# The first block's queries in two halves by heads, one load of a round's last keys with a filled upper half, and a new early order

## The chip, the cores and the metric

The kernel runs on one core of one Trainium2 chip. The metric is the device time of one execution in microseconds (us). Three executions of the kernel before took 822.5, 821.15 and 820.46 us; the median is 821.15. TensorE (PE, with its weight loads as PEld), VectorE (DVE), ScalarE (ACT) and GpSimd (POOL) each run their own queue of instructions in order; SyncE (SP) issues most of the loads and all stores. A change of less than 0.3% (2.5 us) can't be told from none here.

## The reference

Three layers follow each other: linear attention, a gated convolution, and a channel mix with a squared ReLU. Batch 8, 576 positions, 8 heads of 64, so a model width of 512; the hidden width is 1024.

```python
q_s = softmax(q, axis=-1)                  # over the 64 values of a head
k_s = softmax(k, axis=2)                   # over the 576 positions
kv  = einsum('bhsd,bhse->bhde', k_s, v)    # 64x64 for each head
x   = einsum('bhsd,bhde->bhse', q_s, kv)   # then (batch, 576, 512)
gate = sigmoid(sum_k conv_w[k] * x shifted by 4 - k)     # 5 taps, causal
y    = (gate * (x @ w_val)) @ w_out
xk, xr = mixes of y and y shifted by one, with mu_k and mu_r
out  = sigmoid(xr @ w_r) * (relu(xk @ w_k)**2 @ w_v)
```

The weights come as 64-bit numbers; the kernel loads them as pairs of 32-bit words and puts a 32-bit number together from each.

## The kernel before

**Blocks.** The 8 x 576 positions are cut into 12 blocks of T = 384. Each block goes through `V` (times w_val, 4 steps), `Y` (w_out), `R` (w_r), `H` (w_k, 8 steps) and `A` (w_v, 8 steps). Block 0 multiplies plain 32-bit numbers (`whole` weights). From block 1 on each operand is split into a high and a low part and three products are summed.

**Rounds.** The keys and values of four heads of one batch element are a round; there are 16. A round loads its keys (`k_load`: 512 positions as 128 x 4, then the last 64) and values (`v_load`), takes the maximum over positions on DVE (`kv_max`, tile `pm`, its last step over the last 64 positions), turns it with PE (`pmT`, reduced to `m`), spreads it over partitions with PE (`mx`), subtracts it on DVE and takes the exponential on ACT (`kv_exp`), and multiplies keys by values on PE (`kv_mm`, tile `kvacc`). A ones column in the values gives the sums (`den`), and DVE writes the 64x64 matrices (`kvf`). The last 64 positions fill half of the 128 partitions; the other half is loaded with the same keys a second time and its values are zeros. So round 0 gives heads 0 to 3 of the first batch element and round 1 heads 4 to 7.

**Queries.** `load_q` loads a block's queries, for block 0 into `came` (768 KB, in one load). `q_exp` and `q_norm` make the softmax of all 8 heads at once: a maximum (`qm`), a subtraction, an exponential on ACT, a sum (`qs`), a reciprocal and a product. `x_turn` turns two heads (`pq` on PE, `q` by ACT), `x_chunk` multiplies them by `kvf` (`px`, then `xf` by ACT), and `x_gate` makes the gate (one step on ACT, four on DVE, a tanh on ACT). There are four chunks, 0 to 3: chunks 0 and 1 need round 0 alone, chunks 2 and 3 need round 1.

**Weights.** 28 chunks of 512 KB come through seven buffers `raw`: six for most, and one for those in `LEFT_WEIGHTS`. A chunk is put together (`decode`) by one instruction on ACT and two on DVE (`raw<-raw`, then `whole<-raw`), and only then is its buffer free for the next load. In blocks 0 and 1 the weights are also split into high and low parts, once.

**Order.** All is written out in the order of the table `FRONT`, up to block 2's queries: `lwout0` loads chunk 0 of w_out, `wout0` decodes it, `swout0` splits it, `lk0`, `max0`, `turn0` and `mm0` are round 0, `qexp.0` is block 0's `q_exp`, `xturn0.0`, `x0.0` and `gate0.0` its chunk 0, `V0.0` its first step of V (`pv`), `gf0.0` the gate's product with it. A scheduler then places each engine's instructions, so the order on an engine can differ from the table. From block 2 on the table `REST` puts the side work behind the main steps. SP issues loads in its own order too, and at most eight loads are out at a time: each waits for the one eight before it.

Of the kernel before, what the change touches and what calls it, by code (L numbers as in the profile page):

```python
# [8 lines left out]
F32 = mybir.dt.float32  # L9
# [3 lines left out]
ALU = mybir.AluOpType  # L13
AX = mybir.AxisListType
# [3 lines left out]

FRONT = (
# [12 lines left out]
).split()  # L34
REST = {
    0: "max0",
# [19 lines left out]

CONV_ON_TENSOR = ()

LEFT_WEIGHTS = "wval1 wout2 wr2 wr3 wk2 wk7 wv2".split()


@with_exitstack
def tile_linear_attention_gated_conv_channel_mix(
# [15 lines left out]
    nc = tc.nc  # L79
    B, H, S, D = q.shape  # L80
# [4 lines left out]
    P = 128  # L85
    NC = DM // P
    NF = DFF // P
    T = 384
    NT = T // P
    NB = B * S // T  # L90
    NS4 = 4
    KT = NS4 * P
    TAIL = S - KT
    NST = NS4 + 1
    HR = 4
# [5 lines left out]
    odd = ctx.enter_context(tc.tile_pool(name="odd", bufs=1))  # L101
    wts = ctx.enter_context(tc.tile_pool(name="wts", bufs=1))
    kvp = ctx.enter_context(tc.tile_pool(name="kvp", bufs=1))
    work = ctx.enter_context(tc.tile_pool(name="work", bufs=1))
# [11 lines left out]
    first = first_ctx.enter_context(tc.tile_pool(name="first", bufs=1))  # L116
# [6 lines left out]
    def f32(ap):  # L123
        return ap.bitcast(F32)
# [81 lines left out]
    def load_weight(n):  # L206
        w, (kc, c0) = CHUNKS[n]
        here = n in LEFT_WEIGHTS
        raw = raws[n] = (first if here else early).tile([P, WC, 2], U32, tag="raw", bufs=1 if here else 6, name="raw")
# [49 lines left out]

    def frame(vt):
        nc.gpsimd.memset(vt[:, :, 0:NS4, D:VW], 1.0)
        nc.gpsimd.memset(vt[:TAIL, :, NS4, D:VW], 1.0)
        nc.gpsimd.memset(vt[TAIL:P, :, NS4, :], 0.0)
# [3 lines left out]
    vt1 = first.tile([P, HR, NST, VW], F32, name="vt1")  # L269
    frame(vt)  # L270
    frame(vt1)

    def k_load(st):
        b, j = st["at"]
        src = k[b, HR * j:HR * (j + 1)]
        t = st["k"] = kt1 if st is rounds[1] else work.tile([P, HR, NST, D], F32, tag="kt", bufs=1, name="kt")
        nc.sync.dma_start(
            t[:, :, 0:NS4, :].rearrange("p h s d -> p h (s d)"),
            src[:, 0:KT, :].rearrange("h (p s) d -> p h (s d)", s=NS4),
        )  # L280
        for p in (0, TAIL):
            nc.sync.dma_start(t[p:p + TAIL, :, NS4, :], src[:, KT:S, :].rearrange("h p d -> p h d"))

    def v_load(st):
        b, j = st["at"]
# [86 lines left out]
    def segments(i):  # L372

        t, o, segs = i * T, 0, []
        while o < T:
            b, s = divmod(t + o, S)
            n = min(T - o, S - s)
            segs.append((o, n, b, s))
            o += n
        return segs  # L380


    def load_q(i):
        qt = work.tile([P, NT, H, D], F32, tag="qt", bufs=1, name="qt")
        if i == 0:
            came = first.tile([P, H, NT, D], F32, name="came")
            nc.sync.dma_start(
                came.rearrange("p h t d -> p h (t d)"), q[0, :, 0:T, :].rearrange("h (p t) d -> p h (t d)", t=NT)
            )
            return qt, came  # L390
        for t in range(NT):
            for o, n, b, s in segments(i):
                lo_, hi_ = max(o, t * P), min(o + n, (t + 1) * P)
                if lo_ < hi_:
                    nc.sync.dma_start(
                        qt[lo_ - t * P:hi_ - t * P, t, :, :],
                        q[b, :, s + lo_ - o:s + hi_ - o, :].rearrange("h p d -> p h d"),
                    )
        return qt, None

    def q_exp(qt, came):
        qm = odd.tile([P, NT * H], F32, tag="qm", bufs=1, name="qm").rearrange("p (t h) -> p t h", t=NT)
        src = qt if came is None else came.rearrange("p h t d -> p t h d")
        nc.vector.tensor_reduce(out=qm, in_=src, axis=AX.X, op=ALU.max)
        nc.vector.tensor_sub(qt, src, qm.rearrange("p t (h o) -> p t h o", o=1).to_broadcast([P, NT, H, D]))
        nc.scalar.activation(qt, qt, AF.Exp)

    def q_norm(qt):
        a = qt.rearrange("p t h d -> p (t h) d")
        n = NT * H  # L410
        qs = odd.tile([P, n], F32, tag="qm", bufs=1, name="qs")
        nc.vector.tensor_reduce(out=qs, in_=a, axis=AX.X, op=ALU.add)
        nc.vector.tensor_scalar_add(qs, qs, EPS)
        nc.vector.reciprocal(qs, qs)
        nc.vector.tensor_mul(a, a, qs.rearrange("p (n o) -> p n o", o=1).to_broadcast([P, n, D]))

    def pair_of(tag, bufs, pool=work):
        return lambda name: tuple(pool.tile([P, T], F32R, tag=tag, bufs=bufs, name=name + x) for x in "hl")
# [3 lines left out]
    def one(tag, bufs, name):  # L422
        return (gatep if tag == "g" else work).tile([P, T], F32, tag=tag, bufs=bufs, name=name)
# [32 lines left out]
            nc.gpsimd.tensor_copy(tail, view[:, g - 1, w - tail.shape[1]:w])  # L456

    def x_turn(st, i, c):
        qt = st["qt"][0]
        pq = ps_t.tile([P, 512], F32, tag="t", name="pq")  # L460
        for t in range(NT):
            nc.tensor.transpose(  # L462
                pq[:, t * P:(t + 1) * P], qt[:, t, 2 * c:2 * c + 2, :].rearrange("p h d -> p (h d)"), f32(ident)
            )
        if i < 2:
            qf, = st["q", c] = (one("q", 2, "q"),)
            if i:
                nc.scalar.copy(qf, pq[:, :T])
            else:
                nc.scalar.copy(  # L470
                    qf.rearrange("c (p t) -> c p t", t=NT), pq[:, :T].rearrange("c (t p) -> c p t", t=NT)
                )
            return
        qh, ql = st["q", c] = q_pair("q")
        nc.scalar.copy(qh, pq[:, :T])
        nc.vector.tensor_sub(ql, pq[:, :T], f32(qh))
# [40 lines left out]
    def x_gate(st, i, c):  # L517
        g = len(segments(i))
        L = T // g
        gx = lambda a: a.rearrange("p (g t) -> p g t", g=g)  # L520
        xv = st["xv", c]
        data = xv[:, :, HALO:]
        gate = work.tile([P, T], F32, tag="gate", bufs=4, name="gate")
        st["gate", c] = gate
        if i == 0 and c in CONV_ON_TENSOR:
            nc.scalar.activation(gate, conv_on_tensor(xv, c), AF.Tanh, scale=0.5)
            return
        nc.scalar.activation(gx(gate), data, AF.Copy, scale=tap(c, HALO))
        for sh in range(1, NTAP):
            nc.vector.scalar_tensor_tensor(  # L530
                out=gx(gate), in0=xv[:, :, HALO - sh:HALO - sh + L], scalar=tap(c, HALO - sh),
                in1=gx(gate), op0=ALU.mult, op1=ALU.add,
            )
        nc.scalar.activation(gate, gate, AF.Tanh, scale=0.5)
# [158 lines left out]

    def attention(i, nxt):
        out = {
            "qload": lambda: nxt.update(qt=load_q(i)), "qexp": lambda: q_exp(*nxt["qt"]), "qnorm": lambda: q_norm(nxt["qt"][0]),
        }
        for c in range(NC):
            out[f"xturn{c}"] = lambda c=c: x_turn(nxt, i, c)
            out[f"x{c}"] = lambda c=c: x_chunk(nxt, i, c)  # L700
            out[f"gate{c}"] = lambda c=c: x_gate(nxt, i, c)
        return out
# [23 lines left out]
    with tc.issue_after(cast.ins):  # L726
        for n in FRONT:
            todo_front.pop(n)()
            if n == START:
                break  # L730
    for n in FRONT[FRONT.index(START) + 1:]:
        todo_front.pop(n)()
# [42 lines left out]
```

## Time and profile before

| | us |
|---|---|
| median of three executions | 821.15 |
| the profiled execution, whole | 820.3 |
| its span, first to last instruction | 818.4 |
| PE busy | 794.6 (97%) |
| DVE busy | 562.3 (69%) |
| ACT busy | 481.3 (59%) |
| POOL busy | 48.8 (6%) |

The span is what the profile's rows add up to; 1.9 us of the profiled execution lie around it. Busy times overlap between engines. On one engine the next instruction can start before the last has ended in the records, so the distance from start to start is what an instruction costs its queue. A product of plain 32-bit numbers has two records on PE.

### The profile page before, as it was taken

Reading aid. Unit: us, or ns where it says so; the run is one execution under the profiler, and the core shown is the slowest. Engines: PE = TensorE matmul, PEld = TensorE weight load, DVE = VectorE, ACT = ScalarE, POOL = GpSimd, SP = SyncE. Lnnn points to the kernel's source line nnn. Section 1 sums busy time; section 2 is a strip of 40 time slices with the busy share of each in tenths; the row PEclk is TensorE's granted clock in tenths of the full one; section 3 lists DMA queues with packets and bytes.
Section 4 is the critical chain, followed back from the end, with each engine's and each line's share of the span. In section 5 each row is a group of like instructions: output and inputs, shape, how many; then the busy total and the mean of one; then the engine's idle time right before and its main releaser. Section 6 shows DMA issues by size and latency. Waiting matters only on the chain.

```text
span 818.4 us, 12130 instructions
## 1 busy us (share of the span) xinstructions
PE 794.6 (97%) x4530; PEld 696.3 (85%) x4530; DVE 562.3 (69%) x1010; ACT 481.3 (59%) x947; POOL 48.8 (6%) x208
## 2 busy tenths in 40 slices
PE   2999999999999999999999999999999999999997
PEld 1545577999989999999999999999999998998996
DVE  6987689997658667577658578568675857653611
ACT  4566579646754755754753763773673674564542
POOL 1110011000000001100000100100000100100000
PEclk9999999999999999999999999999999999999999
DMA  9685250322032012111241211211213002000001
GB/s 323 199 270 190 61 140 1 76 64 62 8 93 90 13 38 75 26 40 50 52 100 40 62 40 39 62 39 39 62 47 80 14 1 52 26 0 14 26 1 39
DMA packets 96872, 54.28 MB, mean 66 GB/s; under 512 B 78354, under 2 KB 88622, under 8 KB 96814
## 3 DMA queue, kind: packets, MB, share of 16 engines
q1 hardware_dynamic: 96768, 53.49, 22.8%
q8 instruction: 35, 0.57, 0.3%
q14 instruction: 23, 0.19, 0.1%
q10 hardware_dynamic: 46, 0.02, 0.0%
HBM read 44.06 MB, written 9.44 MB: 65 GB/s over the span
## 4 chain that ended last, share of the span: by engine, by line
PE 93%; DVE 3%; DMA 2%; ACT 1%; issue 0%; SPq 0%; DVEq 0%
PE ph L435 25%; PE vacc L435 25%; PE racc L435 12%; PE py L435 11%; PE pv L435 11%; PE px L435 3%; PE kvacc L340 3%; PE pq L462 2%; DMA raw<-in_moe_w_k_dram 1%; DMA came<-in_q_dram 1%; DVE gate L530 1%; DMA raw<-in_moe_w_r_dram 1%; PE mx L326 0%; PE pmT L314 0%; DVE gf L571 0%
## 5 line engine op out<-in xcount | busy, mean ns | idle before, releaser
L435 PE MATMUL ph<-xkh,wk_hi 128*128 128x384 f32 x352 | 120.9, 344 | 0.0
L530 DVE SCALAR_TENSOR_TENSOR gate<-xf,cw,gate 128x384 f32<-128x384 f32 x192 | 117.2, 615 | 3.5 <-issue 0.8
L435 PE MATMUL ph<-xkh,lower 128*128 128x384 f32 x352 | 118.4, 336 | 0.0
L435 PE MATMUL ph<-xkl,wk_hi 128*128 128x384 f32 x352 | 118.4, 336 | 0.0
L428 DVE TENSOR_TENSOR kl<-rf,kh 128x384 fp32r<-128x384 f32 x88 | 48.9, 555 | 87.2 <-ACT kh L427 86.1
L624 ACT ACTIVATE rf<-ph 128x384 f32<-128x384 f32 x96 | 46.9, 490 | 98.6 <-PE ph L435 98.2
L435 PE MATMUL vacc<-wv_hi,kh 128*128 128x512 f32 x264 | 104.2, 395 | 0.0
L435 PE MATMUL vacc<-lower,kh 128*128 128x512 f32 x264 | 103.2, 391 | 0.0
L435 PE MATMUL vacc<-wv_hi,kl 128*128 128x512 f32 x264 | 102.8, 391 | 0.0
L598 DVE SCALAR_TENSOR_TENSOR xm<-yf,mus,xm 128x384 f32<-128x384 f32 x96 | 56.8, 615 | 25.3 <-ACT xm L597 24.8
L435 PEld LDWEIGHTS ph<-xkh,wk_hi 128*128 128x128 f32 x352 | 66.2, 188 | 2.1
L435 PEld LDWEIGHTS ph<-xkh,lower 128*128 128x128 f32 x352 | 66.2, 188 | 1.8
L435 PEld LDWEIGHTS ph<-xkl,wk_hi 128*128 128x128 f32 x352 | 66.1, 188 | 0.0
L435 PE MATMUL py<-gh,wout_hi 128*128 128x384 f32 x176 | 59.9, 347 | 1.8 <-DVE gf L571 1.8
L435 PE MATMUL pv<-xh,wval_hi 128*128 128x384 f32 x176 | 59.4, 338 | 0.0
L435 PE MATMUL pv<-xh,lower 128*128 128x384 f32 x176 | 59.3, 337 | 0.0
L435 PE MATMUL pv<-xl,wval_hi 128*128 128x384 f32 x176 | 59.0, 337 | 0.0
L435 PEld LDWEIGHTS vacc<-wv_hi,kl 128*128 128x128 f32 x264 | 49.5, 188 | 11.0 <-DVE kl L428 0.3
L435 PE MATMUL py<-gh,lower 128*128 128x384 f32 x176 | 58.0, 336 | 0.0
L435 PE MATMUL py<-gl,wout_hi 128*128 128x384 f32 x176 | 57.6, 337 | 0.0
L597 ACT ACTIVATE xm<-yf,mus 128x384 f32<-128x384 f32 x96 | 55.8, 613 | 2.3 <-DVE xrl L428 0.9
L435 PEld LDWEIGHTS vacc<-wv_hi,kh 128*128 128x128 f32 x264 | 49.6, 188 | 8.1 <-ACT kh L427 0.3
(129 smaller groups left out, 1644.8 us busy)
## 6 DMA issues: line engine op xcount, KB each, us to landing
out_dram<-rs SPq DMA_DIRECT2D x36, 256.0 KB, 2.0
kt<-in_k_dram SPq DMA_DIRECT2D x16, 512.0 KB, 4.5
qt<-in_q_dram SPq DMA_DIRECT2D x29, 256.0 KB, 3.7
vt<-in_v_dram SPq DMA_DIRECT2D x56, 128.0 KB, 3.6
raw<-in_moe_w_k_dram SPq DMA_DIRECT2D x8, 512.0 KB, 7.3
raw<-in_moe_w_v_dram SPq DMA_DIRECT2D x8, 512.0 KB, 4.8
raw<-in_moe_w_out_dram SPq DMA_DIRECT2D x4, 512.0 KB, 3.7
kt<-in_k_dram SPq DMA_DIRECT2D x32, 64.0 KB, 4.0
```

Source lines behind the costliest of these rows:

```text
L340: nc.tensor.matmul(acc[e * D:(e + 1) * D, x * VW:(x + 1) * VW], lhsT=kt[:, 2 * x + e, s, :], rhs=st["v"][:, 2 * x + e, s, :], start=(s == ...
L428: nc.vector.tensor_sub(pair[1], a, f32(pair[0]))
L435: nc.tensor.matmul(po, lhsT=left[a], rhs=right[b], start=start and x == 0, stop=stop and x == len(m) - 1)
L462: nc.tensor.transpose(pq[:, t * P:(t + 1) * P], qt[:, t, 2 * c:2 * c + 2, :].rearrange("p h d -> p (h d)"), f32(ident))
L530: nc.vector.scalar_tensor_tensor(out=gx(gate), in0=xv[:, :, HALO - sh:HALO - sh + L], scalar=tap(c, HALO - sh), in1=gx(gate), op0=ALU.mult ...
L597: nc.scalar.activation(gx(xf), yv[:, :, 0:L], AF.Copy, scale=om[:, c:c + 1])
L598: nc.vector.scalar_tensor_tensor(out=gx(xf), in0=yv[:, :, 1:], scalar=mu[:, c:c + 1], in1=gx(xf), op0=ALU.mult, op1=ALU.add)
L624: nc.scalar.activation(rf, ph[:, :T], AF.Relu)
```

## The change

Block 0's queries are loaded by two loads of four heads each (`qload0.0`, `qload1.0`, 384 KB), and `q_exp` and `q_norm` run once for heads 0 to 3 and once for heads 4 to 7 (`qexp0.0`, `qnorm0.0`, `qexp1.0`, `qnorm1.0`). Later blocks keep all heads at once. The last 64 keys of a round are loaded once, into the lower half; POOL fills the upper half with -3.0e38, whose exponential is zero. `LEFT_WEIGHTS` names other chunks, and `FRONT` is a new table (a part of its first line is shown). Line numbers below are those of each kernel.

```diff
-    "lwout0 lk0 qload.0 lk1 max0 cload lv0 lv1 lwval0 lwval1 lwval2 lwval3 lwout1 lwr0 lwout2 lwout3 qexp.0 turn0 "
+    "qload.0 qload0.0 lk0 cload lwval0 lwval1 lk1 lv0 lv1 lwval2 qload1.0 lwout0 lwout1 lwval3 lwr0 max0 turn0 lwout3 "
...
-LEFT_WEIGHTS = "wval1 wout2 wr2 wr3 wk2 wk7 wv2".split()
+LEFT_WEIGHTS = "wval1 wr0 wk1 wk5 wv2".split()
...
+    LEAST = -3.0e38
...
-        for p in (0, TAIL):
-            nc.sync.dma_start(t[p:p + TAIL, :, NS4, :], src[:, KT:S, :].rearrange("h p d -> p h d"))
+        nc.sync.dma_start(t[:TAIL, :, NS4, :], src[:, KT:S, :].rearrange("h p d -> p h d"))
+        nc.gpsimd.memset(t[TAIL:P, :, NS4, :], LEAST)
...
+    def load_half(st, j):
+        h = slice(j * HR, (j + 1) * HR)
+        nc.sync.dma_start(
+            st["came"][:, h].rearrange("p h t d -> p h (t d)"),
+            q[0, h, 0:T, :].rearrange("h (p t) d -> p h (t d)", t=NT),
+        )
+
+    def q_exp(st, h=slice(0, H)):
+        n = h.stop - h.start
+        qt = st["qt"][:, :, h, :]
+        src = st["came"].rearrange("p h t d -> p t h d")[:, :, h, :] if "came" in st else qt
+        qm = odd.tile([P, NT * n], F32, tag=f"qm{n}", bufs=1, name="qm").rearrange("p (t h) -> p t h", t=NT)
...
+    def q_norm(st, h=slice(0, H)):
...
+        if i == 0:
+            for j in range(2):
+                h = slice(j * HR, (j + 1) * HR)
+                out[f"qload{j}"] = lambda j=j: load_half(nxt, j)
+                out[f"qexp{j}"] = lambda h=h: q_exp(nxt, h)
+                out[f"qnorm{j}"] = lambda h=h: q_norm(nxt, h)
```

On PE, from round 0's product of keys and values (`kvacc<-vt,kt`) to the first products of block 0's V (`pv`), there stood before:

```order
L340 MATMUL kvacc<-vt,kt 64x65 x20
L314 MATMUL pmT<-ident,pm 128x128 x2
L326 MATMUL mx<-ident,m_249 128x128 x2
L462 MATMUL pq<-ident,qt 128x128 x3
L435 MATMUL px<-q,kvf_116 128x384
L340 MATMUL kvacc<-vt_124,kt_123 64x65 x20
L462 MATMUL pq<-ident,qt 128x128 x3
L435 MATMUL pv<-xf,whole 128x384
```

And on the same engine now, a little further on:

```order
L344 MATMUL kvacc<-vt,kt 64x65 x20
L473 MATMUL pq<-ident,qt 128x128 x6
L318 MATMUL pmT<-ident,pm 128x128 x2
L446 MATMUL px<-q,kvf_116 128x384 x2
L330 MATMUL mx<-ident,m_264 128x128 x2
L177 MATMUL pc<-ident,cwt 128x20
L446 MATMUL pv<-xf,whole 128x384
L180 MATMUL pm<-ident,mut 128x8
L446 MATMUL pv<-xf,whole 128x384 x4
L344 MATMUL kvacc<-vt_124,kt_123 64x65 x20
L446 MATMUL pv<-xf,whole 128x384 x3
L473 MATMUL pq<-ident,qt 128x128 x6
```

Chunks 0 and 1 (two `px`) and five products of V moved ahead of round 1's `kvacc<-vt_124,kt_123`; the small transposes of the constants (`pc`, `pm`), which were ahead of round 0, moved behind it.

On ACT, around round 0's exponential (`kt<-kt`) and the copies of the two rounds' values (`vt<-dense`, `vt_124<-dense`), there stood before:

```order
L406 ACTIVATE qt<-qt 128x1536
L176 COPY cw<-pc 128x20
L299 COPY vt<-dense 128x4x4x64
L180 COPY mus<-pm 128x8
L330 ACTIVATE kt<-kt 128x1280
L299 COPY vt_124<-dense 128x4x4x64
L146 ACTIVATE raw<-raw 128x512 x3
```

And now:

```order
L148 ACTIVATE raw<-raw 128x512 x2
L416 ACTIVATE qt<-qt 128x3x256
L303 COPY vt<-dense 128x4x4x64
L303 COPY vt_124<-dense 128x4x4x64
L334 ACTIVATE kt<-kt 128x1280
L148 ACTIVATE raw<-raw 128x512
```

Round 1's copy of values moved ahead of round 0's exponential, and two weight chunks ahead of the queries' exponential, which is for half of the heads.

On DVE, from the sums of round 0 (`den<-kvacc`) to the second round's subtraction (`kt_123<-kt_123,mx`), there stood before:

```order
L347 TENSOR_SCALAR den<-kvacc 128x2
L316 TENSOR_REDUCE m_249<-pmT 128x2
L348 RECIPROCAL den<-den 128x2
L147 TENSOR_SCALAR raw<-raw 128x512
L352 TENSOR_TENSOR kvf_116<-kvacc,den 64x2x64 x2
L327 TENSOR_TENSOR kt_123<-kt_123,mx 128x1280
```

And now:

```order
L351 TENSOR_SCALAR den<-kvacc 128x2
L414 TENSOR_REDUCE qm<-came 128x12
L352 RECIPROCAL den<-den 128x2
L415 TENSOR_TENSOR qt<-came,qm 128x3x256
L356 TENSOR_TENSOR kvf_116<-kvacc,den 64x2x64 x2
L320 TENSOR_REDUCE m_264<-pmT 128x2
L149 TENSOR_SCALAR raw<-raw 128x512
L423 TENSOR_REDUCE qs<-qt 128x12
L149 TENSOR_SCALAR raw<-raw 128x512
L331 TENSOR_TENSOR kt_123<-kt_123,mx 128x1280
```

The second half of the queries now stands between `den` and `kvf`, and behind it; round 1's `m` moved behind `kvf`.

## Rows read from the trace of the kernel before

**Rows 1.** The page: span, and busy time of each engine (share, instructions).

```profile
span 818.4 us, 12130 instructions
PE 794.6 (97%) x4530; PEld 696.3 (85%) x4530; DVE 562.3 (69%) x1010; ACT 481.3 (59%) x947; POOL 48.8 (6%) x208
```

**Rows 2.** Stretches from:to: length; PE, PEld, DVE, ACT, POOL; clock, DMA share, GB/s.

```profile
0.00:27.20 27.20, 11.12 (x98) 7.70 (x99) 18.82 (x37) 12.73 (x19) 4.72 (x28) 1.00 0.86 286
27.20:800.00 772.80, 769.36 (x4368) 676.86 (x4367) 539.72 (x968) 464.49 (x920) 44.06 (x180) 1.00 0.21 59
```

**Rows 3.** A wait of PE in the span: us in total, times, longest.

```profile
PE py L435 <- DVE gf L571: 2.2, 2, 1.8
```

**Rows 4.** PE in order of time: start, us, line, op, tiles, records, idle before.

```profile
16.65 2.44 PE L340 MATMUL kvacc<-vt,kt 128*64 128x65 f32 x40 [2.10 <-issue]
...
22.60 1.65 PE L435 MATMUL px<-q,kvf 128*128 128x384 f32 x2 [0.57 <-ACT q L470]
...
26.54 0.90 PE L462 MATMUL pq<-ident,qt 128*128 128x128 f32 x3
27.24 1.21 PE L435 MATMUL pv<-xf,whole 128*128 128x384 f32 x2
28.28 0.81 PE L435 MATMUL px<-q,kvf 128*128 128x384 f32 x2
...
35.40 5.32 PE L435 MATMUL pv<-xf,whole 128*128 128x384 f32 x16
40.55 5.32 PE L435 MATMUL py<-gf,whole 128*128 128x384 f32 x16
46.26 5.43 PE L435 MATMUL py<-gf,whole 128*128 128x384 f32 x16 [0.38 <-DVE gf L571]
...
52.49 10.57 PE L435 MATMUL racc<-whole,xm 128*128 128x512 f32 x24 [0.59 <-DVE xm L598]
```

**Rows 5.** DVE in order of time, 8 to 53 us.

```profile
8.89 1.75 DVE L404 TENSOR_REDUCE qm<-came 128x24 f32<-128x1536 f32 x1 [1.18 <-DMA came<-in_q_dram]
...
13.76 1.49 DVE L327 TENSOR_TENSOR kt<-kt,mx 128x1280 f32<-128x1280 f32 x1
...
20.49 0.58 DVE L352 TENSOR_TENSOR kvf<-kvacc,den 64x128 f32<-64x128 f32 x2
...
30.61 2.73 DVE L530 SCALAR_TENSOR_TENSOR gate<-xf,cw,gate 128x384 f32<-128x384 f32 x5 [0.24 <-ACT gate L528]
...
35.06 1.29 DVE L148 SCALAR_TENSOR_TENSOR whole<-raw 128x512 uint32<-128x512 uint32 x2
...
45.65 1.02 DVE L571 SCALAR_TENSOR_TENSOR gf<-gate,pv 128x384 f32<-128x384 f32 x2 [1.58 <-ACT gate L534]
46.58 0.69 DVE L148 SCALAR_TENSOR_TENSOR whole<-raw 128x512 uint32<-128x512 uint32 x1
...
51.49 0.43 DVE L147 TENSOR_SCALAR raw<-raw 128x512 uint32<-128x512 uint32 x1 [0.35 <-DMA raw<-in_moe_w_r_dram]
51.83 0.61 DVE L598 SCALAR_TENSOR_TENSOR xm<-yf,mus,xm 128x384 f32<-128x384 f32 x1
```

**Rows 6.** ACT in order of time, 15 to 23 us.

```profile
15.28 1.27 ACT L330 ACTIVATE kt<-kt 128x1280 f32<-128x1280 f32 x1
16.45 1.03 ACT L299 COPY vt<-dense 128x1024 f32<-128x1024 f32 x1
...
22.07 0.48 ACT L470 COPY q<-pq 128x384 f32<-128x384 f32 x1 [2.87 <-PE pq L462]
```

**Rows 7.** SP's issues: round 1's values, and the last chunk of w_r.

```profile
8.88 0.37 SPq L290 DMA_DIRECT2D dense<-in_v_dram  x1
...
47.33 0.33 SPq L210 DMA_DIRECT2D raw<-in_moe_w_r_dram  x1
```

**Rows 8.** From issue to landing: the values, then the page's row on w_k.

```profile
DMA to landing us min/median/max: 5.6/5.6/5.7
...
raw<-in_moe_w_k_dram SPq DMA_DIRECT2D x8, 512.0 KB, 7.3
```

**Rows 9.** POOL in order of time, one fill of the zero half.

```profile
3.83 0.31 POOL L265 MEMSET vt<- 64x260 f32 x1
```

More of the change, by code (lines that the diff above doesn't have):

```diff
@@ L380, in segments, with load_q @@
         return segs
-    def load_q(i):
-        qt = work.tile([P, NT, H, D], F32, tag="qt", bufs=1, name="qt")
+    def load_q(i, st):
+        st["qt"] = work.tile([P, NT, H, D], F32, tag="qt", bufs=1, name="qt")
         if i == 0:
[L386 to L390, printed above, removed]
+            st["came"] = first.tile([P, H, NT, D], F32, name="came")
+            return
         for t in range(NT):
@@ L395, in load_q @@
                     nc.sync.dma_start(
-                        qt[lo_ - t * P:hi_ - t * P, t, :, :],
+                        st["qt"][lo_ - t * P:hi_ - t * P, t, :, :],
                         q[b, :, s + lo_ - o:s + hi_ - o, :].rearrange("h p d -> p h d"),
                     )
[L399 to L403, printed above, removed]
+    def load_half(st, j):
[9 more added lines that the diff above has]
+        qm = odd.tile([P, NT * n], F32, tag=f"qm{n}", bufs=1, name="qm").rearrange("p (t h) -> p t h", t=NT)
         nc.vector.tensor_reduce(out=qm, in_=src, axis=AX.X, op=ALU.max)
-        nc.vector.tensor_sub(qt, src, qm.rearrange("p t (h o) -> p t h o", o=1).to_broadcast([P, NT, H, D]))
+        nc.vector.tensor_sub(qt, src, qm.rearrange("p t (h o) -> p t h o", o=1).to_broadcast([P, NT, n, D]))
         nc.scalar.activation(qt, qt, AF.Exp)
[L408 to L412, printed above, removed]
+    def q_norm(st, h=slice(0, H)):
+        n = h.stop - h.start
+        qt = st["qt"][:, :, h, :]
+        qs = odd.tile([P, NT * n], F32, tag=f"qm{n}", bufs=1, name="qs")
+        q4 = qs.rearrange("p (t h) -> p t h", t=NT)
+        nc.vector.tensor_reduce(out=q4, in_=qt, axis=AX.X, op=ALU.add)
         nc.vector.tensor_scalar_add(qs, qs, EPS)
         nc.vector.reciprocal(qs, qs)
-        nc.vector.tensor_mul(a, a, qs.rearrange("p (n o) -> p n o", o=1).to_broadcast([P, n, D]))
+        nc.vector.tensor_mul(qt, qt, q4.rearrange("p t (h o) -> p t h o", o=1).to_broadcast([P, NT, n, D]))
     def pair_of(tag, bufs, pool=work):
@@ L458, in x_turn @@
     def x_turn(st, i, c):
-        qt = st["qt"][0]
+        qt = st["qt"]
         pq = ps_t.tile([P, 512], F32, tag="t", name="pq")
@@ L695, in attention @@
         out = {
-            "qload": lambda: nxt.update(qt=load_q(i)), "qexp": lambda: q_exp(*nxt["qt"]), "qnorm": lambda: q_norm(nxt["qt"][0]),
+            "qload": lambda: load_q(i, nxt), "qexp": lambda: q_exp(nxt), "qnorm": lambda: q_norm(nxt),
         }
+        if i == 0:
[4 more added lines that the diff above has]
+                out[f"qnorm{j}"] = lambda h=h: q_norm(nxt, h)
         for c in range(NC):
```

23 rows, old and new, of the table FRONT are left out of this document.

## The prediction

> **What bounds the kernel now.** I read the busy row of each engine first: PE is busy for 794.6 of the span's 818.4 us, DVE for 562.3 [rows 1]. Next the stretches, to see where PE's missing time lies: up to 27.2 us PE works for 11.12 us, while from 27.2 to 800 us it works for 769.36 of 772.80 [rows 2]. So the idle time to be won is some 16 us at the front. Of the 3.4 us idle behind 27.2 us, the waits put 2.2 on Y's product waiting for DVE's `gf`, in two places, 1.8 in the longer one (block 1) [rows 3], and 0.59 stands in front of R [rows 4]. Last I read the engines in order of time. PE works on `kvacc` at 16.65, the first `px` at 22.60, the first V product at 27.24, Y at 40.55, R at 52.49 [rows 4]. From there on it is full. The change leaves every matrix product as it was, so its worth is how much earlier or later R starts, if nothing new stands still behind that.
>
> One more thing is to be seen. A `px` of two records took 1.65 us at 22.60 and 0.81 us at 28.28 [rows 4]: half the time, as between TensorE's lower level (1.2 GHz) and its upper (2.4). It rose between those two, after PE had worked without a pause since 22.60. At the upper level eight products go from 35.40 to 40.55, 0.645 us each [rows 4].
>
> **The change part by part.**
>
> *Loads and values.* The first steps of round 0 need its keys, and both kernels must wait for values. The loads issued ahead of round 1's values are, before, 512 + 640 + 768 + 640 + 576 KB; now 384 + 576 + 1024 + 576 + 576 KB; both sums are 3136 KB. Round 1's values were issued at 8.88 [rows 7] and took 5.6 [rows 8], so they landed at 14.5, and I take 14.5 again. What is new is that ACT copies them (1.03 [rows 6]) ahead of round 0's exponential, to 15.5; the exponential takes 1.17 until the next instruction starts [rows 6], so `kvacc` starts at 16.7. It started at 16.65: no gain. Bounds: without the copy in the way, the exponential follows DVE's subtraction, which ended at 15.2 [rows 5]. DVE now handles half of the queries ahead of it but also two steps on a weight chunk; I estimate 14.1 at best, hence `kvacc` from 15.5. If the values land 1 us later, 17.7.
>
> *Queries in halves.* A full `qm` takes 1.75 us for 1536 elements, a subtraction 1.49 for 1280 [rows 5]; by that slope 768 elements take 0.97, by half of 1.75 it is 0.88. Four such DVE steps in two halves each therefore add 0 to 0.8 us, and most of it falls into time in which DVE waits. What counts is where the second half stands: its `qm` and its subtraction now lie between `den` and `kvf`. `kvacc` ends at 16.7 + 2.4 = 19.1; then 0.1 + 0.9 + 0.1 + 0.9 + 0.6 gives `kvf` at 21.7. Before, it ended at 20.49 + 0.58 = 21.1 [rows 5]: 0.6 later.
>
> *Chunks 0 and 1 ahead of round 1's `kvacc`.* Both are turned (`pq` 0.7 us at the lower level [rows 4], the copy 0.48 [rows 6]) while DVE makes `kvf`. PE then has `pmT` (0.7), two `px` at 1.6 each and `mx` (0.7): the first V product starts at 21.7 + 0.7 + 3.2 + 0.7 + 0.1 = 26.4, against 27.24. That is 0.8 earlier, but round 1's `kvacc` (2.4 before) is still to do, and one `px` and one `pq` (0.65 + 0.35 at the upper level) are done already.
>
> *Where it goes.* `kvacc` of round 1 waits for its exponential, which stands on ACT behind the constants' copies, two gate steps and a weight chunk and, on DVE, behind an `mx` that PE reaches only at 25.6. I get the exponential's end at about 30.6. The five products of V ahead of it last from 26.4 to 30.9 if two of them go at the lower level, so PE stands still hardly at all. `kvacc` then ends at 32.2, its three V products at 34.2, `kvf` of round 1 at about 34.1, `pq` and `px` of chunks 2 and 3 with their copies at 36.5, eight products more at 41.7; without the pauses that I see for the copies, 41.1. V ended at 40.55 before. So V is 0.5 to 1.1 us later.
>
> *Y and R.* Y's third row waited until 46.26 for two `gf` [rows 4, 5], 0.56 beyond 40.55 + 5.15. DVE now has put two chunks fewer together by then (a `whole` step is 0.65 [rows 5], so 1.3 us less, and as much more for their first steps); a gate step stays 0.55 [rows 5]. I expect `gf` at 45.0 and Y's third row without a wait, since V ends later by itself. Y ends at 41.1 to 41.7 + 10.3 = 51.4 to 52.0 (before 51.5). R stood behind Y's end by about 0.95, which is the way over ACT and DVE's `xm` at 51.83; I take 0.75, since the step on a w_r chunk that held DVE to 51.83 [rows 5] has moved. R starts at 52.15 to 52.75, and I take 52.3: **0.2 us earlier**.
>
> *Last keys.* Of two loads of 64 KB a round one goes, and a POOL fill of 64 x 256 comes, about 0.31 us by the fill of 64 x 260 [rows 9]; 16 x 0.31 = 5 us on an engine with 48.8 us of work [rows 1]. It waits for the buffer as the load did, and stands ahead of the exponential by whole blocks from round 2 on; in rounds 0 and 1 it runs while the keys are on their way. Price 0; if its cover were gone, 0.31 a round.
>
> *Later blocks.* A few small PE groups stand some products earlier. PE is full there; 0 to 0.3 us either way, taken as 0. Block 1's wait of 1.8 for `gf` stays.
>
> *Sum.* 818.4 - 0.2 = 818.2 in the span, and with the 1.9 around it 820.1. The profiled execution took 820.3, 0.85 under the median, so against the median it is 820.95, say **820.9**.
>
> **The rivals.**
>
> *Faster: an early exponential.* If the values land earlier than at 14.5 because fewer small loads share the queues, `kvacc` starts at 15.5, `kvf` is there at 20.5, PE works without a pause from there, the upper level comes before the second `px` (0.8 saved), and V starts at 24.4. As round 1's exponential moves along, R starts at 50.3 to 49.6: 2.2 to 2.9 less, 818.2 to 818.9. For it: DVE and ACT have less ahead of the exponential. Against it: the same bytes ahead of the values, and a DMA share of 0.86 in this stretch [rows 2].
>
> *Slower: a w_k chunk in R's way.* DVE's first step on wk1 now stands ahead of the first `xm`, and ACT's ahead of the second. Its load goes out when wr0 has been put together, about where that `whole` step was, at 46.6 [rows 5]. The last w_r chunk before was issued at 47.33 [rows 7] and its DVE step waited to 51.49 [rows 5], 4.2; the w_k loads took 7.3 [rows 8]. So it lands at 50.8 or at 53.9. It decides from 51.3 on; at 53.9 the first `xm` comes 2.6 later, R starts at about 55.0, and the time is 823.6. I am nearer to 4.2, because in the new order few loads are out at that time.
>
> *Slower: the level stays low.* What the row shows is that the level rose behind a stretch with `px`, `kvacc` and `pq` [rows 4]. The new stretch from 21.7 holds a larger part of turning. If PE still had the lower level for the five V products, they would cost 1.3 instead of 0.65, 3.2 us more for the five; two of them I had at that level already, so 2 us more, 822.9, and up to 3.2, 824.1, if the products behind `kvacc` are slow too. (The Trainium skill, "TensorE: Matmul & The Clock Gate", "Part 4: PE-mode transpose", says that transposes do not count as busy for the clock in the way that products do; by that rule this case would hold. The trace here has both kinds mixed in front of the rise and doesn't settle it.)
>
> *The change does nothing for the front.* If PE's pauses only change places, R starts at 52.5 and the time is 821.1. It lies inside the forecast.
>
> **How the numbers follow.** The forecast, with the case before this line, 0.56; faster 0.24; the chunk in the way 0.12; the low level 0.08. About 0.3%, 2.5 us, is what a measurement can tell here, so the bounds are 818.65 and 823.65. The faster rival lies on both sides of the first, two thirds of it below; with a little of the forecast's own tail that is 0.19. Beyond the second lie half of the chunk's rival (7.3 is a median), half of the low level, and 0.05 of the forecast's tail for weights of H that come late, since one buffer now serves five chunks where it served seven: 0.15. Within: 0.66. The range goes from 818.3, which leaves out about a tenth, to 823.6, which leaves out 0.10 or a little more at the other end.
>
> **What would show it.** Right: `kvacc` at 16.7, the first V product near 26.4, round 1's `kvacc` near 31, V's end near 41.4, Y without a wait in its third row, R near 52.3. `kvacc` at 15.5 and V's first product under 25 would show the faster rival. A wait of DVE for w_k's load near 51 us in front of `xm` shows the first slower one; V products of 1.3 us behind 28 the second. Wrong altogether would be a new wait of PE behind R, for a weight chunk in H or A.

## The result, and the profile after

Five executions of the changed kernel took 824.28 to 826.59 us, median 826.33, against 821.15 before (five executions, 820.46 to 822.5): a ratio of 1.0056, 95% interval [1.0041, 1.007]. It is slower by 0.56%, outside the predicted range of 818.3 to 823.6. The profiled execution took 826.59, of which 824.8 are the span; that is 6.4 more than the span before [rows 1]. The medians lie 5.2 apart; the profiled execution of before is 0.85 under its median. What follows takes the 6.4 apart.

The page of the changed kernel, span and busy time of each engine:

```profile
span 824.8 us, 12147 instructions
PE 799.3 (97%) x4530; PEld 697.5 (85%) x4530; DVE 563.7 (68%) x1016; ACT 481.2 (58%) x948; POOL 57.0 (7%) x224
```

PE has as many instructions as before and is busy 4.7 us longer. So most of the 6.4 us isn't idle time. The waits of PE from 15 us on, over 1 us (total, times, longest), as [rows 3] were before:

```profile
PE kvacc L344 <- ACT kt L334: 4.7, 1, 4.7
PE racc L446 <- DVE xm L609: 1.9, 1, 1.9
PE py L446 <- DVE gf L582: 1.8, 1, 1.8
```

Y's wait in block 0 is gone (`gf` once instead of twice), and R has a wait of 1.9 where it had 0.59. PE in order of time in the front (start, us, idle before in brackets), to be laid beside [rows 4]:

```profile
17.30 2.44 PE L344 MATMUL kvacc<-vt,kt 128*64 128x65 f32 x40 [4.67 <-ACT kt L334]
...
23.09 2.77 PE L446 MATMUL px<-q,kvf 128*128 128x384 f32 x4
25.65 0.43 PE L330 MATMUL mx<-ident,m 128*128 128x128 f32 x2
...
26.18 0.91 PE L446 MATMUL pv<-xf,whole 128*128 128x384 f32 x2
...
27.17 2.85 PE L446 MATMUL pv<-xf,whole 128*128 128x384 f32 x8
29.95 1.39 PE L344 MATMUL kvacc<-vt,kt 128*64 128x65 f32 x40
...
35.84 5.43 PE L446 MATMUL pv<-xf,whole 128*128 128x384 f32 x16
41.11 10.48 PE L446 MATMUL py<-gf,whole 128*128 128x384 f32 x32
51.43 0.38 PE L318 MATMUL pmT<-ident,pm 128*128 128x128 f32 x2
53.72 2.84 PE L446 MATMUL racc<-whole,xm 128*128 128x512 f32 x6 [1.91 <-DVE xm L609]
```

Up to Y's end the main starts of the front lie near the predicted ones. Then PE stands before R. What it waits for is seen on DVE, and on SP, which issued the load:

```profile
52.71 0.43 DVE L149 TENSOR_SCALAR raw<-raw 128x512 uint32<-128x512 uint32 x1 [1.70 <-DMA raw<-in_moe_w_k_dram]
53.05 0.61 DVE L609 SCALAR_TENSOR_TENSOR xm<-yf,mus,xm 128x384 f32<-128x384 f32 x1
```

```profile
46.48 2.24 SPq L212 DMA_DIRECT2D raw<-in_moe_w_k_dram  x3
```

DVE's first step on a w_k chunk stands ahead of `xm` and waits until 52.7 for its load, the first of these three, issued at 46.48. R starts at 53.72 instead of 52.49: **1.23 us**. Of these, 0.56 were there when Y started (41.11 for 40.55), as the prediction had it. From Y's start to R's it took 12.61 us for 11.94 before, although Y's own wait was gone.

**The other 5.2 us come behind R.** The starts of R cut the span into block lengths. From the first R to the last, before took 720.01 (52.49 to 772.50) and after 725.28 (53.72 to 779.00), 5.27 more. From there to PE's end it is 0.24 more, and the stores behind PE take 0.37 less: 1.23 + 5.27 + 0.24 - 0.37 = 6.37. PE is full there in both, but for the 1.8 us in block 1. Two things happened.

First, **the same products take longer.** R of block 2, from its first product to the first of H, in the kernel before and then in the changed one:

```profile
198.32 0.39 PE L435 MATMUL racc<-wr_hi,xrh 128*128 128x512 f32 x1
...
206.49 0.34 PE L435 MATMUL ph<-xkh,wk_hi 128*128 128x384 f32 x1
```

```profile
199.87 0.39 PE L446 MATMUL racc<-wr_hi,xrh 128*128 128x512 f32 x1
...
208.28 0.34 PE L446 MATMUL ph<-xkh,wk_hi 128*128 128x384 f32 x1
```

8.17 against 8.41 us for 36 products, without a pause. The lines view, two of R's three kinds of product over the whole span (count | busy us, mean ns), before and after:

```profile
L435 PE MATMUL racc<-wr_hi,xrh 128*128 128x512 f32 x132 | 51.5, 390 | 0.0
L435 PE MATMUL racc<-lower,xrh 128*128 128x512 f32 x132 | 51.4, 390 | 0.0
```

```profile
L446 PE MATMUL racc<-wr_hi,xrh 128*128 128x512 f32 x132 | 52.5, 398 | 0.0
L446 PE MATMUL racc<-lower,xrh 128*128 128x512 f32 x132 | 52.5, 397 | 0.0
```

From block 2 on R went from 8.17 to 8.42 in every block; V and Y, where no small group stands in them, went from 8.34 to 8.42 and from 8.47 to 8.55. H (16.92) and A (16.55) stayed.

Second, blocks 2, 5 and 8, counted from the start of R to that of the next block's R, grew by 0.9 where their neighbours grew by 0.3 to 0.4. One `kvacc` group in block 2, before and after:

```profile
259.59 1.39 PE L340 MATMUL kvacc<-vt,kt 128*64 128x65 f32 x40
```

```profile
259.61 0.45 PE L344 MATMUL kvacc<-vt,kt 128*64 128x65 f32 x6
259.99 0.62 PE L446 MATMUL py<-gl,wout_hi 128*128 128x384 f32 x2
260.53 1.26 PE L344 MATMUL kvacc<-vt,kt 128*64 128x65 f32 x34
```

The group is cut in two by two products of Y, and `mx` moved from Y into V, where only `pmT` had stood.

### The profile page after: what moved, and what is told of

Read it like the earlier page. It is cut to its first block, busy times and chain, and to the rows that moved or that the text cites. A ratio compares the mean times of both kernels' runs of the same rounds, so it can differ in the third digit from the quotient of the medians.

```text
span 824.8 us, 12147 instructions
## 1 busy us (share of the span) xinstructions
PE 799.3 (97%) x4530; PEld 697.5 (85%) x4530; DVE 563.7 (68%) x1016; ACT 481.2 (58%) x948; POOL 57.0 (7%) x224
## 4 chain that ended last, share of the span: by engine, by line
PE 95%; DMA 2%; DVE 2%; ACT 0%; issue 0%; SPq 0%
PE ph L446 25%; PE vacc L446 25%; PE racc L446 13%; PE pv L446 12%; PE py L446 11%; PE px L446 4%; PE kvacc L344 3%; PE pq L473 2%; DMA dense<-in_v_dram 1%; DMA raw<-in_moe_w_k_dram 1%; DMA kt<-in_k_dram 1%; DVE gate L541 1%; PE pmT L318 0%; DVE gf L582 0%; PE mx L330 0%
## 5 line engine op out<-in xcount | busy, mean ns | idle before, releaser
L609 DVE SCALAR_TENSOR_TENSOR xm<-yf,mus,xm 128x384 f32<-128x384 f32 x96 | 56.3, 614 | 17.1 <-ACT xm L608 16.7
L438 ACT CAST gh<-gf 128x384 fp32r<-128x384 f32 x44 | 22.4, 510 | 65.5 <-DVE gf L582 65.5
L487 DVE TENSOR_TENSOR ql<-pq,qh 128x384 fp32r<-128x384 f32 x40 | 22.2, 554 | 50.3 <-ACT qh L486 50.3
```

The costliest lines, as they stand in the source:

```text
L438: nc.scalar.copy(pair[0], a)
L609: nc.vector.scalar_tensor_tensor(out=gx(xf), in0=yv[:, :, 1:], scalar=mu[:, c:c + 1], in1=gx(xf), op0=ALU.mult, op1=ALU.add)
```

## The experiments

**What differs in the products.** The change gave the queries' maxima and sums a size of their own for the halves: a second tile of 12 columns (48 bytes in each partition), where there was one tile of 24 columns (96 bytes). By the addresses in the compiled kernels, the low parts of all weights moved by 64 bytes (the first from 32256 to 32320), and so did the operands that they meet and the high parts of w_k (169728 to 169792) and w_v; all these lie on the left. The high parts of w_val, w_out and w_r, on the right, stayed (from 204544). Those three weights belong to V, Y and R. The kernel has pad tiles at four places (`left_gap` 96 bytes, `before_gap` 64, `behind_gap` 192, `right_gap` 224), which shift the tiles behind them, so each of these can be tried on the kernel before.

The theory: the **distance** between the tiles on the left and those on the right, which the products of a stage read in turn, sets their pace. Rivals: a tile's own address does; or the order of the groups does it all. The span of each kernel's profiled execution was cut at the starts of R: R of block 0 (the front), to R of block 1 (block 0), and from there to R of block 11 (the later blocks), in us. Three kernels ran once and have no ratio.

| kernel | based on | median | ratio to before [95%] | front | block 0 | later blocks |
|---|---|---|---|---|---|---|
| before | | 821.15 | | 52.49 | 80.25 | 639.76 |
| after | | 826.33 | 1.0056 [1.0041, 1.007] | 53.72 | 80.33 | 644.95 |
| e1_one_tile | after | 820.77 | 0.9997 [0.9984, 1.0009] | 51.96 | 80.26 | 641.46 |
| e2_gap_160 | before | 825.39 | 1.0044 [1.0029, 1.0059] | 51.96 | 82.16 | 643.39 |
| e3_one_tail | before | 824.51 | 1.0039 [1.0025, 1.0054] | 54.27 | 80.32 | 641.43 |
| e4_wk1_late | after | 826.22 | 1.0056 [1.004, 1.0072] | 53.54 | 80.35 | 644.97 |
| e5_both_gaps | before | 823.05 | 1.0024 [1.0012, 1.0037] | 52.86 | 80.29 | 641.55 |
| e6_wk1_early | e1 | 822.47 | 1.0008 [0.9995, 1.0021] | 50.26 | 81.79 | 641.44 |
| e7_two_loads_later | e1 | 822.64 | 1.0015 [1.0, 1.0029] | 53.51 | 83.47 | 639.81 |
| e8_copy_on_pool | e1 | 820.55 | 0.998 [0.9963, 0.9996] | 51.84 | 80.26 | 641.44 |
| e9_together | e1 | 821.85 | 1.0011 [1.0002, 1.0021] | 48.45 | 82.22 | 639.85 |
| e10_work_side | before | 829.57 | | 52.70 | 80.34 | 647.96 |
| e11_gated_at_0 | before | 824.57 | 1.0051 [1.0031, 1.0072] | 52.31 | 80.82 | 643.05 |
| e12_right_side | before | 823.58 | | 51.79 | 80.34 | 643.42 |
| e13_four_near | e1 | 818.59 | 0.9969 [0.9957, 0.9982] | 50.78 | 81.83 | 639.81 |
| e14_gap_224 | before | 822.91 | | 51.39 | 81.85 | 641.76 |
| e15_distance_kept | before | 822.27 | 1.0015 [1.0004, 1.0026] | 52.15 | 80.58 | 639.80 |

The last column repeats to 0.1 between kernels that share a cause, while the columns before it move by some 2 us. So the later blocks are what tells, and the median, which has the front and block 0 in it, follows them only in part.

**One tile again.** The halves use the first 12 columns of one 24-column tile; the order on every engine stays as changed.

```diff
-        qm = odd.tile([P, NT * n], F32, tag=f"qm{n}", bufs=1, name="qm")...
+        qm = odd.tile([P, NT * H], F32, tag="qm", bufs=1, name="qm")[:, 0:NT * n]...
```

> The changed kernel, with the sums and maxima of the queries in one tile of 24 columns as before, of which a half uses the first 12. Every engine's order is that of the changed kernel, but the weights and all behind them lie 64 bytes lower, where they lay before the change. Theory placement: the products of split numbers in R (8.42 us a block now, 8.17 before), V and Y (0.07 and 0.08 more) slowed because their tiles moved by 64 bytes; R falls back to 8.17 a block, and some 4 us go: 822.3. Rival order: the slower products come from what the other engines do beside them (POOL's fills, the moved small groups); R stays at 8.42 and the time at 826.3.

R of block 2 takes 8.17 again:

```profile
197.95 0.39 PE L446 MATMUL racc<-wr_hi,xrh 128*128 128x512 f32 x1
...
206.12 0.34 PE L446 MATMUL ph<-xkh,wk_hi 128*128 128x384 f32 x1
```

The later blocks take 641.46: 3.5 of the 5.2 us are gone, and the kernel is level with before. Blocks 2, 5 and 8 still take 65.77 instead of 65.29. So the second tile, two lines of the change, costs 3.5 us in these blocks, and the rest is something else.

**The same shift in the kernel before.**

```diff
-LEFT_GAP, RIGHT_GAP = 96, 224
+LEFT_GAP, RIGHT_GAP = 160, 224
```

> The kernel before with LEFT_GAP at 160 bytes instead of 96, so that the weights and all behind them lie 64 bytes higher; nothing else, and every engine's order is the same. Theory placement: R goes from 8.17 to 8.42 us a block in blocks 2 to 11, V and Y by 0.07 and 0.08, together about 0.4 a block and 4 us: 825.1. Rival order: no difference, 821.15.

Nothing of the change is in this kernel but 64 bytes of pad, and it has the products of after. R of block 2:

```profile
199.87 0.39 PE L435 MATMUL racc<-wr_hi,xrh 128*128 128x512 f32 x1
...
208.29 0.34 PE L435 MATMUL ph<-xkh,wk_hi 128*128 128x384 f32 x1
```

8.42; V 8.42 and Y 8.55; the later blocks 3.63 above before. Placement is a cause by itself.

**Distance, or the address itself?** Four more pads: both sides (`160, 288`; a larger `RIGHT_GAP` moves the right side down, so the tiles come 128 bytes nearer), the right side alone (`96, 288`), the left by 128 (`224, 224`), and both by 64 the same way (`160, 160`).

> The kernel before with LEFT_GAP at 160 and RIGHT_GAP at 288 bytes: the tiles on both sides move by 64 bytes, so the high parts of w_val, w_out and w_r, which lie on the right, keep their place against the low parts and the operands on the left; order unchanged. Theory relative: what counts is how the tiles of a product lie against each other in steps of 128 bytes; R comes back to 8.17 us a block and the time to 821.2. Theory absolute: a tile that doesn't begin at a multiple of 128 is slow; R stays at 8.42 or grows, and the time is 825.4 or more.

> The kernel before with RIGHT_GAP at 288: only the high parts of w_val, w_out and w_r (and the raw buffers) move by 64 bytes. Theory relative: high and low parts of these three mix again, as in e2 with the signs turned; R 8.42, V and Y 0.07 to 0.1 more, H and A unchanged. Rival, only the operands on the left count: nothing changes, R 8.17.

> The kernel before with LEFT_GAP at 224, 128 bytes more than before and 64 more than e2. Theory: only the place in steps of 128 bytes counts, so R is back at 8.17 us a block and V at 8.34. Rival: any move on the left against the right costs, R stays at 8.42 or grows.

> The kernel before with LEFT_GAP at 160 and RIGHT_GAP at 160: the tiles on the left lie 64 bytes higher, as in e2, and those on the right lie 64 bytes higher too (in e5 they went down, which made the distance 128), so all tiles move together. Theory distance: only how the tiles of a product lie against each other counts; R 8.17 us a block, V 8.34, Y 8.47, the time 821.2. Rival place: a tile's own offset counts; R 8.25 to 8.42 as in e2, e5 and e14, and 823 or more.

e5 was meant to keep the distance, but its sign was wrong, so its expectation describes e15's case; it came out between (R 8.25, V 8.43, Y 8.47). The other three separate the theories. With 64 bytes from the right side alone the later blocks take 643.42, as with 64 from the left (643.39). With 128 from the left alone they take 641.76, near e5's 641.55. With both moved the same way they take 639.80, as before. R of block 2 with 64 from the right (e12), with 128 from the left (e14), then with the distance kept (e15):

```profile
197.90 0.39 PE L435 MATMUL racc<-wr_hi,xrh 128*128 128x512 f32 x1
...
206.32 0.34 PE L435 MATMUL ph<-xkh,wk_hi 128*128 128x384 f32 x1
```

```profile
198.96 0.40 PE L435 MATMUL racc<-wr_hi,xrh 128*128 128x512 f32 x1
...
207.21 0.34 PE L435 MATMUL ph<-xkh,wk_hi 128*128 128x384 f32 x1
```

```profile
198.37 0.39 PE L435 MATMUL racc<-wr_hi,xrh 128*128 128x512 f32 x1
...
206.54 0.34 PE L435 MATMUL ph<-xkh,wk_hi 128*128 128x384 f32 x1
```

8.42, 8.25 and 8.17. So it is how left and right lie against each other, tried here at three distances and one common shift. (e15's median is 1.9 above its before, 820.38, though the profiled execution has the products and the span, 818.4, of before; what the other executions spend isn't explained.)

It isn't the distance of a product's own two tiles alone. `racc<-lower,xrh` has both on the left, 64 bytes on in e2 like each other, and it slowed most: from its start to the next product's, 227.0 ns before and 236.8 in e2 (means over R of blocks 2 to 11). `racc<-wr_hi,xrh`, which the low part follows, went from 226.6 to 235.5, and `racc<-wr_hi,xrl`, which another high part follows, only from 227.2 to 230.1. In V it is alike: 173.5 to 175.8 and 174.1 to 177.2 where high and low parts take turns, 174.1 to 173.4 where a high part follows a high part. With 64 bytes more, the slow places in R and V are those where one product's weights lie on one side and the next one's on the other.

**Other distances.** e10 takes e2 and leaves `before_gap` out, so that the low parts and the other operands move by 64 bytes, while the gated operands (of Y and H) and the high parts of all weights stay; e11 leaves the sides and moves `before_gap` from 64 to 128 bytes and `behind_gap` from 192 to 128.

> The kernel before with LEFT_GAP at 160 and the 64 bytes of before_gap left out: low parts, xh, xl, xr, kh and kl move by 64 bytes; the gated operands (gh, gl, xkh, xkl) and the high parts of all weights stay. Theory relative: every stage now mixes high parts at 0 and low parts at 64; R 8.42 us a block and V 8.42 as in e2, and H and A, which never changed so far, slow down too (H above 16.92, A above 16.55). Rival, the moved operand alone counts: R and V as in e2, H and Y as before.

> The kernel before with only the gated operands (gh, gl, xkh, xkl) moved by 64 bytes, to multiples of 128 as all the others: before_gap 128 bytes, behind_gap 128. Theory relative: Y and H become like V, where all operands begin at multiples of 128; 8.34 for 48 products where Y takes 8.47 and H 16.92 for 96; so Y 8.34, H 16.7, some 0.35 a block and 3.8 us less: 817.3. Rival: the offset of the gated operands is good as it is, and Y and H stay or grow: 821.2 or more.

I hoped for a gain from e11 and lost 3.3 us: Y 8.47 to 8.57, H 16.92 to about 17.1. e10 has H at 17.13 and, alone of all, A at 16.80. In these two kernels too, stages whose tiles lie otherwise against each other change their pace, but I have no rule that says which distance is good.

**One load of the last keys, alone**, in the kernel before.

```diff
-        for p in (0, TAIL):
-            nc.sync.dma_start(t[p:p + TAIL, :, NS4, :], src[:, KT:S, :].rearrange("h p d -> p h d"))
+        nc.sync.dma_start(t[:TAIL, :, NS4, :], src[:, KT:S, :].rearrange("h p d -> p h d"))
+        nc.gpsimd.memset(t[TAIL:P, :, NS4, :], -3.0e38)
```

> The kernel before with the single load of a round's last keys and POOL's fill, nothing else by hand; the placement of tiles is that of before, and the scheduler puts the small groups of blocks 2, 5 and 8 elsewhere by itself. Theory placement: R stays at 8.17; only the moved groups cost, 0.5 us in each of three blocks: 822.6. Rival fills: POOL's 16 fills beside the products slow R, V and Y, R comes to 8.42 and the time to 825. Third, the part costs nothing: 821.15.

No product changes, and blocks 2, 5 and 8 take 65.77: the later blocks 1.67 above before, of which 3 x 0.48 = 1.45 lie in these. R stays at 8.17, so POOL's fills don't slow the products. So the single load, and not the new early order, moves the groups there. Alone it also costs 1.78 at the front. ACT in this kernel, then PE:

```profile
14.47 1.98 ACT L299 COPY vt<-dense 128x1024 f32<-128x1024 f32 x2
...
18.36 1.27 ACT L330 ACTIVATE kt<-kt 128x1280 f32<-128x1280 f32 x1 [0.76 <-issue]
```

```profile
19.69 2.43 PE L340 MATMUL kvacc<-vt,kt 128*64 128x65 f32 x40 [2.85 <-ACT kt L330]
```

Both copies stand ahead of the exponential here too, and `kvacc` starts 3.0 later than at 16.65.

**The reverse: two loads where they don't stand at the front** (e1, with the second load again from round 2 on).

> The changed kernel with the one tile of e1, and from round 2 on the second load of the last keys as before instead of POOL's fill. Theory: the scheduler puts pmT, mx and kvacc of blocks 2, 5 and 8 back where they were, kvacc is one piece again, and each of the three blocks takes 65.3 us instead of 65.77: 1.45 less than e1, 819.3. Rival: the three blocks' 0.48 comes from the fills and loads themselves and not from the place: blocks stay at 65.77 or the time at 820.8.

The later blocks fall to 639.81, before's time. But the order in block 0 then has round 2's maximum late, and block 0 takes 83.47, with this wait and with the fall of the clock that e6 shows below:

```profile
77.15 0.43 PE L333 MATMUL mx<-ident,m 128*128 128x128 f32 x2 [1.23 <-DVE m L323]
```

**The w_k chunk in R's way.** e4 moves `wk1` in the table behind the steps `y1.0` to `y3.0`. e6 (on e1) takes `wr0` out of `LEFT_WEIGHTS`, so that wk1's buffer is free earlier.

> The changed kernel with wk1 put together behind all of block 0's mixes instead of amid them, so that neither ACT nor DVE waits for its load ahead of the first xm. Theory: R starts at 52.3 to 52.6 instead of 53.72 and nothing behind it stands still, so 1.2 us go: 825.1. Rival: the wait comes back, because wk1 and the chunks behind it are put together later than H needs them; PE then stands still in H, and the time stays at 826.3 or grows.

> The changed kernel with the one tile of e1, and wr0 out of LEFT_WEIGHTS, so that wk1's buffer is free when wval1 has been put together and its load goes out ten microseconds earlier; neither DVE nor ACT then has a weight chunk whose load is late ahead of the first xm. Theory: R starts 0.3 to 1.2 us earlier than in e1 and the changed kernel (51.96 and 53.72), right behind Y: 820.0 to 820.5. Rival: wr0 now takes one of the six buffers, other chunks come later, and the wait moves to them: 820.8 or more.

e4 changed nothing, because the table isn't the order on DVE: the step on the chunk still stood ahead of `xm`, and the wait is still there.

```profile
52.53 0.43 DVE L149 TENSOR_SCALAR raw<-raw 128x512 uint32<-128x512 uint32 x1 [1.09 <-DMA raw<-in_moe_w_k_dram]
```

In e6 PE doesn't wait for `xm`: from Y's start to R's it takes 11.02 us, where the changed kernel takes 12.61 and e1, whose chunk landed earlier, 11.26. R starts at 50.26, 1.7 before e1's 51.96, but 1.45 of that was there at Y's start (39.24 for 40.69). The time didn't follow (822.47); in the profiled execution the gain is lost in block 0, 81.79 for 80.26. In block 1 PE waits 1.83 for `gf`, as it did before [rows 3]; here TensorE's granted clock fell behind that. Windows (from:to; PE, PEld, DVE, ACT, POOL; clock, DMA share, GB/s):

```profile
120.00:122.00 2.00, 0.80 (x5) 0.48 (x3) 2.00 (x6) 2.00 (x5) 0.06 (x1) 1.00 0.00 0
122.00:124.00 2.00, 1.36 (x7) 1.33 (x8) 2.00 (x6) 2.00 (x6) 0.16 (x1) 0.85 0.00 0
124.00:126.00 2.00, 2.00 (x9) 1.90 (x8) 2.00 (x3) 1.11 (x3) 0.00 (x0) 0.50 0.00 0
126.00:128.00 2.00, 2.00 (x11) 2.00 (x11) 1.74 (x3) 1.11 (x2) 0.19 (x1) 0.80 0.00 0
```

0.50 is the lower level, 1.2 GHz. In the profiled execution of before the same pause left the clock at 1.00. e2 and e14 have before's order of work, and there the clock fell behind it as well, to 0.50 from 126 to 128 us; their block 0 is the longer by it (82.16 and 81.85).

**Round 1's values copied by POOL** (on e1), so that ACT's exponential isn't behind them.

```diff
-        nc.scalar.copy(st["v"][:, :, 0:NS4, 0:D], st["dense"])
+        if st is rounds[1]:
+            nc.gpsimd.tensor_copy(st["v"][:, :, 0:NS4, 0:D], st["dense"])
+        else:
+            nc.scalar.copy(st["v"][:, :, 0:NS4, 0:D], st["dense"])
```

> The changed kernel with the one tile of e1, and POOL copies round 1's values instead of ACT, so that nothing stands ahead of round 0's exponential but the copy of its own values. Theory early exponential: kvacc starts 1.2 to 1.9 us earlier than it would, at 15.5 to 17, V's first product at about 25, R 1 us earlier or more: 819.0 to 819.8. Rival: V's first product hangs on what stands behind kvacc, the level of TensorE's clock and the second half of the queries ahead of kvf, and PE only waits longer there: 820.8.

```profile
15.68 2.44 PE L347 MATMUL kvacc<-vt,kt 128*64 128x65 f32 x40 [2.94 <-ACT kt L337]
...
24.35 0.91 PE L449 MATMUL pv<-xf,whole 128*128 128x384 f32 x2
...
51.84 2.41 PE L449 MATMUL racc<-whole,xm 128*128 128x512 f32 x5 [1.85 <-DVE xm L612]
```

That is the early exponential of the prediction's faster rival, with `kvacc` at 15.68 and V at 24.35. Y starts 1.41 earlier than in e1, and 1.3 of it is lost again to the w_k chunk in front of R: 51.84.

**Together.** e9 is e1 with e6, e7 and e8; e13 the same, with one load and a fill in rounds 0 to 3 and two loads from round 4 on.

> The changed kernel with what e1, e6, e7 and e8 took away one by one: one tile, wk1's load early, two loads of the last keys from round 2 on, round 1's values copied by POOL. Theory: the costs add up, so R starts near 50 with no wait for a weight chunk, blocks 2, 5 and 8 take 65.3 us, R 8.17: 817 to 818.5, less than both kernels. Rival: what is won at the front is given back in block 0 or 1, by chunks that come late or by a spell at TensorE's lower level: 820 or more.

> e9 with the single load and POOL's fill in rounds 0 to 3 and two loads from round 4 on, so that mx of round 2 stands again behind the first vacc of block 0 where it had no wait (it waited 1.6 us in e9, 1.2 in e7). Theory: block 0 takes 80.3 us from R to R instead of 82.2 and the front's gain stays, R near 48.5 and the time 816 to 818. Rival: the gain goes elsewhere, most of all where PE waits 1.8 us for gf in block 1 and the clock falls behind it: 820 or more.

e9 has R at 48.45, but `mx` of round 2 waits 1.55 in block 0, and only 2 of 13 executions came out near 818. In e13 `mx` of round 2 is in time again. R is at 50.78, not at the 48.5 that I expected, and the later blocks at 639.81; over 12 executions it is **faster than both kernels**, 0.3% under before: 0.9969 [0.9957, 0.9982]. Its executions at a mean granted clock of 1.0 took 816.3 to 817.9, six of the seven others 819.3 to 820.3. Its profile has the fall in block 1 too: Y of block 1, from its first product to R's, takes 12.45 us there with its wait, and 10.88 in before and in e1.

## Why the prediction was wrong

**Right at the front.** V's first product was to start at 26.4 and did at 26.18. V's end was to come at 41.1 to 41.7 and came at 41.11. Y has no wait in its third row. `kvacc` came at 17.30, not 16.7: the copy of the values started at 15.03, which is 0.5 later than I let them land. The low level didn't stay: the products of V from 27.17 took (29.95 - 27.17) / 4 = 0.70 each. So the rule on transposes cited with that rival (the Trainium skill, "TensorE: Matmul & The Clock Gate", Part 4) didn't decide here. The granted clock reads 1.00 through the front in both kernels [rows 2], so the levels there are read from the products' pace alone.

V's start came right by luck: two errors cancel. `px` began at 23.09, 0.7 later than my sum has it (21.7 + 0.7), and the two took 2.56 (to 25.65) where I put 3.2: I had taken a record of 1.65 for what a `px` costs PE, but from start to start it was 1.28.

**Wrong at R.** I put R at 52.3, on the ground that a w_r chunk's step no longer held `xm`. A w_k chunk's step took its place. That was the second of my four rivals, and I gave it 0.12 because I took the landing to be near 4.2 us behind the issue. It was 6.2 (46.5 to 52.7), between my 4.2 and 7.3, and landing after 51.3 it decided. I let 11.05 pass from Y's start to R's (10.3 + 0.75), and it was 12.61. The term was -0.2 and measured +1.23.

**Wrong behind R, and this is most of it.** "The change leaves every matrix product as it was" failed, and with it "later blocks: 0 to 0.3, taken as 0". That term measured 5.2 in the later blocks. About 3.5 of it is the second small tile (e1 against after), the same as 64 bytes of pad alone (e2, 3.63). About 1.7 is the single load of the last keys (e3), which I had costed as POOL's 0.31 a round, hidden. It was hidden on POOL; what cost was that the small groups were placed at other points of PE's order (e7 puts them back and has before's later blocks, 639.81). I had seen that they moved and took it for free, as PE is full there. The two add up: 1.67 + 3.63 = 5.3, against 5.19 measured. Without this term R's 1.23 alone would have left the time inside the range. I did read the added tile and looked for what its instructions cost, but not for what lies behind it in memory.

**Open.** Why the distance between left and right changes the pace of products, and why Y and H are faster with the gated operands 64 bytes off than without (e11). What makes R in e1 start 1.76 before the changed kernel's: the chunk landed 1.8 earlier, and I have one profile of each. An order with `xm` ahead of the chunk's step on DVE wasn't reached.

## What to carry to other kernels

Where a stage is at the pace of TensorE, compare the time per product of a stage before and after, not only waits: 7 ns per product of R, 36 products in each of 10 blocks, are 2.5 us that no wait shows. A new tile, here of 48 bytes, can move all tiles behind it; keep sizes and tags, or compare the addresses of the operands that meet. A side group that moves within a full PE has a price too, and a table of steps tells where a step stands on an engine only after the scheduler has placed it.

## What the runs showed of the hardware

- The pace of back-to-back products depends on how far the tiles that they read in turn lie from each other in a partition. R's 36 products took 8.17 us, with 64 bytes more between left and right 8.42, with 128 more 8.25, and 8.17 where both sides moved by 64. V took 8.34, 8.42 and 8.43, Y 8.47, 8.55 and 8.47.
- A group of forty 128x65 records cut in two by two products of Y costs PE about 0.25 us more by its own starts (`kvacc` per block in blocks 2, 5 and 8: 2.64 and 2.89 for two rounds), and the products around it lose some as well: in e1 the whole Y took 10.29 us with the cut group (block 2) and 9.91 with a group in one piece (block 3).
- After a pause of PE of 1.8 us the granted clock fell to 0.50 in some executions and stayed at 1.00 in others of the same order of work (before against e2 and e14). Block 0 took 81.8 to 82.2 us with the fall (e2, e6, e13, e14) and 80.2 to 80.4 without it (before, after, e1, e5, e10, e12).
